# Top-k attention and a hard-swish feed-forward in one kernel: transposing a unit's weights three steps after its scores, and feed-forward pieces of half the size

## Chip, cores and metric

The kernel runs on one core of one Trainium2 chip. The metric is the time on the device in microseconds (us) of one execution. Of a kernel's plain runs the median counts; one more execution is recorded by the profiler, and its own time stands beside it.

TensorE is the matrix engine (PE in the profile, its weight loads PEld), VectorE is DVE, ScalarE is ACT, GpSimd is POOL, and SyncE (SP) issues the transfers.

## What is computed

Attention over 8 batches, 8 heads, 576 positions and a head dimension of 64, where each row keeps the scores that reach its 32nd largest; then a feed-forward on 4608 rows of 512, with 2048 inner columns. All in 32-bit floats (the inputs lie in 64-bit floats for the feed-forward's weights, and the kernel converts these itself).

```python
scores = scale * np.matmul(q, k.transpose(0, 1, 3, 2))
kth = np.partition(scores, -32, axis=-1)[..., -32:-31]
scores = np.where(scores >= kth, scores, -1e9)
attn = np.exp(scores - np.max(scores, axis=-1, keepdims=True))
attn = attn / (np.sum(attn, axis=-1, keepdims=True) + 1e-09)
x = np.matmul(attn, v)            # (B,H,S,D) -> (B*S, H*D)
h = x @ w_in
out = (h * np.clip(h + 3.0, 0.0, 6.0) / 6.0) @ w_out
```

## The kernel before

**Units.** The heads go in pairs, four pairs a batch. A pair's 576 rows are four blocks of 128 rows and a rest of 64. A *full* unit is one block of 128 rows for both heads of a pair: two score tiles of 128 x 576. A *rest* unit is the rest of 64 rows of both heads, which lie above one another in the partitions: one tile of 128 x 576. There are 128 full and 32 rest units, 160 in all, in groups of five: four full ones (one for each pair, the same block) and a rest one, which stands last in even batches and first in odd ones.

**What happens to a unit.** `scores` (L206 for a rest unit, L213 for a full one) multiplies on TensorE into `big`, and ScalarE copies it out (L208, L214, L217). `top` finds the 32 largest of each row on VectorE: four rounds of `max` (L230), with three of `match_replace` (L234) between them, which write the work buffer `wk`. `mask` compares and adds on GpSimd (L244, L249) and makes the shift (L252). `exp` is ScalarE's exponential with its running sum (L257), and GpSimd adds a small constant to the sum, `den` (L262). `weights` takes the reciprocal on VectorE (L266) and scales on ScalarE (L268). `transpose` turns the weights on TensorE into `big` (L279), and ScalarE copies them to `eT` (L281). `values` multiplies with v into a PSUM tile `pv` (L291), for a full unit together with that of the neighbour, and ScalarE copies it out (L409). After the fourth full unit of a group, 128 rows of x are whole and a feed-forward tile is put on the list `todo`; the rest units give one such tile for every two batches. So there are 36 feed-forward tiles.

**Shared buffers.** `big` is one PSUM tile of four banks; scores, weights' transposes and the transposes of a new pair's q and k (`pT` below, L178, L180, copied out at L183, L184) take turns in it. The other four PSUM banks are a pool (`ps_w`) for the feed-forward's `h` and `acc`, for `pv` and for the conversion's `f`. There are four score tiles `sc` and two `wk`.

**Feed-forward in pieces.** A tile of 128 rows is a generator with eight pieces: four that each compute 512 columns of h (16 matmuls, L308), ScalarE's rectifier (L316) and, delayed to the next piece, VectorE's gate (L320); then four that each add four of the sixteen products into `acc` (L327), the last with ScalarE's scaling (L337) and the store. `piece()` runs the next one, if `todo` holds one.

**Order.** The order is written out by hand; each engine works through its list in that order. In step n stand, for TensorE: scores of unit n+1; a piece; transposes of unit n-2; a piece (not if unit n is a rest unit); perhaps a pair's transposes; `values`; and at every fourth step one more piece. For VectorE: the reciprocal of unit n-2, then the four rounds of unit n, with gates between them. For ScalarE: the scaling of unit n-2 behind the copy of the scores of n+1, and the exponential of unit n-1 at the end. For GpSimd: the sum of unit n-1, then the mask of unit n. The first eight steps (EARLY) differ: there a unit is finished one step later, and the weights of the feed-forward are loaded and converted from 64-bit to 32-bit floats (`convert`, L99 to L122), one chunk of 32 at each of four calls in a step. A call finishes the oldest chunk under way if two are, and starts the next. The tile names in this program are the ones that the trace prints.

Of the kernel before, what the change touches and what calls it, by code (L numbers as in the profile page):

```python
# [26 lines left out]
def kernel(  # L27
# [16 lines left out]
    NHP = H // 2  # L44
# [5 lines left out]
    def pool(name, bufs, **kw):  # L50
        return ctx.enter_context(tc.tile_pool(name=name, bufs=bufs, **kw))
# [1 line left out]
    consts = pool("consts", 1)  # L53
    ldpool = pool("ld", 2)
    kqpool = pool("kq", 2 * NHP)
    scpool = pool("sc", 4)
    wkpool = pool("wk", 2)
    mpool = pool("m", 4)
    etpool = pool("et", 2)
# [64 lines left out]
    def weight_chunks():  # L124
        win, wout = moe_w_in.bitcast(U32), moe_w_out.bitcast(U32)
        for f in range(0, FF, WC):
            for g in range(NHP):
                rows = slice(g * P, (g + 1) * P)
                yield w_in[:, g, f : f + WC], win[rows, 2 * f : 2 * (f + WC)]
        for c in range(NFC):  # L130
            rows = slice(c * P, (c + 1) * P)
            yield w_out[:, c, :], wout[rows, :]
# [168 lines left out]
    def feed_forward(xT, rows):  # L301

        gs = []
        for f0 in range(0, NFC, 4):
            h = ps_w.tile([P, 512], F32, tag="w", name="h")
            for f in range(f0, f0 + 4):
                for i in range(NHP):
                    nc.tensor.matmul(  # L308
                        h[:, (f - f0) * P : (f - f0 + 1) * P],
                        w_in[:, i, f * P : (f + 1) * P],  # L310
                        xT[:, i, :],
                        start=(i == 0),
                        stop=(i == NHP - 1),
                    )
            g = gpool.tile([P, 512], F32, tag="g", name="g")
            nc.scalar.activation(g[:], h[:], AF.Relu, bias=three[:], scale=1.0)  # L316
            gs.append(g)

            def gate(g=g, h=h):
                nc.vector.scalar_tensor_tensor(  # L320
                    out=g[:], in0=g[:], scalar=6.0, in1=h[:], op0=ALU.min, op1=ALU.mult
                )

            yield gate
        acc = ps_w.tile([P, DM], F32, tag="w", name="acc")
        for f in range(NFC):
            nc.tensor.matmul(  # L327
                acc[:],
                gs[f // 4][:, (f % 4) * P : (f % 4 + 1) * P],
                w_out[:, f, :],  # L330
                start=(f == 0),
                stop=(f == NFC - 1),
            )
            if f % 4 == 3:
                if f == NFC - 1:
                    o = opool.tile([P, DM], F32, tag="o", name="o")
                    nc.scalar.mul(o[:], acc[:], 1.0 / 6.0)  # L337
                    for p0, p1, dst in rows:
                        nc.sync.dma_start(dst, o[p0:p1, :])
                yield None  # L340
# [5 lines left out]
    pairs = {(b, hp): Pair(b, hp) for b in range(B) for hp in range(NHP)}  # L346
    units = []
    for b in range(B):
        for qt in range(J):
            full = [Unit(pairs[b, hp], qt) for hp in range(NHP)]  # L350
# [3 lines left out]
    per_batch = NHP * (J + 1)  # L354
    NU = len(units)
    todo = []
    gate = None

    def run_gate():
        nonlocal gate  # L360
        if gate:
            gate()
        gate = None

    def piece():
        nonlocal gate
        run_gate()
        while todo:
            try:
                gate = next(todo[0])  # L370
                return
            except StopIteration:
                todo.pop(0)

    chunks = list(weight_chunks())
    converting = []

    def convert_step():

        if converting and (len(converting) > 1 or not chunks):  # L380
            next(converting.pop(0), None)
        if chunks:
            c = convert(*chunks.pop(0))
            next(c)
            converting.append(c)

    EARLY = 8
    state = {}

    def values(n):  # L390
# [30 lines left out]
    def pair_at(n, first):  # L421

        b, at = divmod(n, per_batch)
        hp, odd = divmod(at - first, 3)
        return pairs[b + 1, hp] if b + 1 < B and not odd and 0 <= hp < NHP else None

    pairs[0, 0].load()
    convert_step()
    pairs[0, 0].transpose()
    units[0].scores()  # L430
    convert_step()
    pairs[0, 1].load()
    convert_step()
    pairs[0, 1].transpose()
    for hp in range(2, NHP):
        pairs[0, hp].load()
    for hp in range(NHP):
        pairs[0, hp].load_values()

    for n in range(NU + 2):  # L440
        early = n < EARLY
        u = units[n] if n < NU else None
        pieces = 2
        if u and u.rest:
            pieces = 1
        if n % 4 == 3 and n > 2 * EARLY:
            pieces += 1
        d = n - (1 if early else 2)
        d = d if 0 <= d < NU and n != EARLY else None
        if n + 1 < NU:  # L450
            units[n + 1].scores()
        if n < 2:
            pairs[0, n + 2].transpose()
        if d is not None and not early:
            units[d].weights()
        if u:
            u.begin()
            u.top(0)
        p = pair_at(n, 6)
        if p:  # L460
            p.load()
            p.load_values()
        convert_step()
        piece()
        if u:
            u.top(1)
        if d is not None:
            if early:
                units[d].exp()
            else:  # L470
                units[d].transpose()
        convert_step()
        if u:
            u.top(2)
        convert_step()
        if d is not None and early:
            units[d].weights()
            units[d].transpose()
        if pieces > 1:
            piece()  # L480
        p = pair_at(n, 8)
        if p:
            p.transpose()
        if d is not None:
            values(d)
        if u:
            u.top(3)
        convert_step()
        for _ in range(2, pieces):
            piece()  # L490
        if not early and 1 <= n < NU + 1:
            units[n - 1].exp()
        if u:
            u.mask()
    while todo:
        piece()
    run_gate()


# [32 lines left out]
```

## Time and profile before

| | us |
|---|---|
| median of 3 runs | 1967.45 |
| lowest and highest | 1967.02, 1968.03 |
| the profiled execution | 1967.0 |
| its span, first to last instruction | 1965.2 |

| engine | busy us | share of the span |
|---|---|---|
| TensorE, matmuls | 1688.6 | 86% |
| TensorE, weight loads | 1237.7 | 63% |
| VectorE | 1551.5 | 79% |
| GpSimd | 1160.5 | 59% |
| ScalarE | 973.6 | 50% |

The mean granted clock of TensorE is 0.933 of full speed. A step takes some 11 us. Busy times overlap; what counts is which engine waits for which, and in which stretch. In the chain that ended last, followed back from the end, TensorE has 78% of the span, GpSimd 9% and ScalarE 8%.

### The profile page before, as it was taken

The numbers are of one execution on the slowest core, as the hardware profiler recorded it, in microseconds if no ns is written. First come the engines' busy times: TensorE is split into PE (matmuls) and PEld (weight loads), VectorE is DVE, ScalarE is ACT, GpSimd is POOL, SyncE is SP. The second block draws the span as 40 slices with busy tenths as digits, with TensorE's granted clock in tenths as the row PEclk, the third lists the DMA queues.
The fourth block names the chain that finished last, engine by engine and source line by source line (L and its number), as shares of the span: only waits on it lengthen the run. The fifth ranks groups of instructions, "written<-read, shape, count | busy, mean of one in ns | idle before, by whom it ended". The sixth has DMA issues, their size and how long they took to land.

```text
span 1965.2 us, 30832 instructions
## 1 busy us (share of the span) xinstructions
PE 1688.6 (86%) x11872; PEld 1237.7 (63%) x11872; DVE 1551.5 (79%) x3249; ACT 973.6 (50%) x1717; POOL 1160.5 (59%) x878
## 2 busy tenths in 40 slices
PE   3346889788999998798899998988899999978899
PEld 2244666556777766566666766666576666665576
DVE  4775897877988777888898778887898888877860
ACT  3553465455554554544544555544554554454541
POOL 3875665656656555665665556555566565555650
PEclk9877899889999999898899999988899999988899
DMA  6340100110001100101001110001001010000000
GB/s 180 117 126 27 45 7 7 42 33 15 1 24 31 39 10 6 43 12 31 7 6 25 30 42 7 25 18 42 7 6 25 25 42 7 6 7 6 6 7 11
DMA packets 101139, 56.53 MB, mean 29 GB/s; under 512 B 84096, under 2 KB 92288, under 8 KB 100992
## 3 DMA queue, kind: packets, MB, share of 16 engines
q1 hardware_dynamic: 100992, 54.55, 10.2%
q8 instruction: 94, 1.54, 0.3%
q14 instruction: 53, 0.43, 0.1%
HBM read 45.09 MB, written 9.44 MB: 28 GB/s over the span
## 4 chain that ended last, share of the span: by engine, by line
PE 78%; POOL 9%; ACT 8%; issue 3%; SPq 1%; DMA 1%; DVE 1%; POOLq 0%; ACTq 0%
PE h L308 26%; PE acc L327 23%; PE pv L291 10%; PE big L279 8%; PE big L213 6%; POOL wk L244 5%; POOL sc L249 3%; ACT sc L257 2%; ACT eT L281 2%; PE big L206 2%; PE big L178 2%; ACT kq L183 1%; ACT sc L214 1%; ACT sc L268 1%; DMA st<-in_moe_w_in_dram 0%
## 5 line engine op out<-in xcount | busy, mean ns | idle before, releaser
L244 POOL TENSOR_SCALAR wk<-sc,m 128x576 f32<-128x576 f32 x288 | 638.1, 2223 | 30.7 <-DVE m L230 19.8
L230 DVE MAX8 m<-wk 128x8 f32<-128x576 f32 x864 | 620.5, 762 | 3.0
L327 PE MATMUL acc<-w_out,g 128*128 128x512 f32 x1152 | 527.8, 603 | 0.0
L308 PE MATMUL h<-xT,w_in 128*128 128x128 f32 x4096 | 488.6, 278 | 0.0
L308 PEld LDWEIGHTS h<-xT,w_in 128*128 128x128 f32 x4096 | 470.2, 193 | 6.2 <-issue 1.3
L234 DVE MATCH_REPLACE8 wk<-m,wk 128x576 f32<-128x576 f32 x576 | 427.4, 756 | 0.0
L262 POOL TENSOR_SCALAR den<-den 128x2 f32<-128x2 f32 (+1 forms) x160 | 37.4, 234 | 632.5 <-ACT sc L257 595.4
L249 POOL TENSOR_TENSOR sc<-sc,wk 128x1152 f32<-128x1152 f32 (+1 forms) x160 | 382.3, 2389 | 13.3
L327 PEld LDWEIGHTS acc<-w_out,g 128*128 128x128 f32 x1152 | 210.5, 192 | 222.7 <-issue 217.0
L279 PE MATMUL big<-ident,sc 128*128 128x128 f32 x1344 | 201.2, 297 | 168.8 <-ACT sc L268 136.3
L279 PEld LDWEIGHTS big<-ident,sc 128*128 128x128 f32 x1344 | 169.4, 154 | 212.6 <-issue 143.1
L257 ACT ACTIVATE sc<-sc,shift 128x576 f32<-128x576 f32 x288 | 221.4, 772 | 118.3 <-POOL shift L252 118.1
L266 DVE RECIPROCAL den<-den 128x2 f32<-128x2 f32 (+1 forms) x160 | 26.5, 165 | 296.3 <-POOL den L262 296.0
L281 ACT COPY eT<-big 128x1152 f32<-128x1152 f32 (+1 forms) x160 | 169.1, 1057 | 128.9 <-PE big L279 128.9
L316 ACT ACTIVATE g<-h,three 128x512 f32<-128x512 f32 x144 | 99.2, 689 | 268.4 <-PE h L308 268.3
L268 ACT ACTIVATE sc<-sc,den 128x576 f32<-128x576 f32 x288 | 210.8, 778 | 26.0 <-DVE den L266 24.8
L213 PE MATMUL big<-kq 64*128 64x512 f32 (+1 forms) x1024 | 182.3, 478 | 40.7 <-ACT eT L281 25.4
L234 DVE MATCH_REPLACE8 wk<-m,sc 128x576 f32<-128x576 f32 x288 | 212.9, 750 | 0.0
L291 PE MATMUL pv<-eT,vm 128*64 128x128 f32 (+1 forms) x2560 | 186.6, 296 | 25.4 <-ACT eT L281 25.4
L230 DVE MAX8 m<-sc 128x8 f32<-128x576 f32 x288 | 204.1, 749 | 3.6 <-ACT sc L217 3.6
L291 PEld LDWEIGHTS pv<-eT,vm 128*64 128x64 f32 x2560 | 156.0, 156 | 60.2 <-ACT eT L281 32.7
L213 PEld LDWEIGHTS big<-kq 64*128 64x128 f32 x1024 | 95.5, 202 | 141.1 <-issue 88.5
(42 smaller groups left out, 1074.6 us busy)
## 6 DMA issues: line engine op xcount, KB each, us to landing
kin<-in_k_dram SPq DMA_DIRECT2D x64, 128.0 KB, 2.9
qin<-in_q_dram SPq DMA_DIRECT2D x64, 128.0 KB, 2.8
st<-in_moe_w_in_dram SPq DMA_DIRECT2D x16, 512.0 KB, 4.2
vm<-in_v_dram SPq DMA_DIRECT2D x64, 128.0 KB, 2.4
st<-in_moe_w_out_dram SPq DMA_DIRECT2D x16, 512.0 KB, 3.7
out_dram<-o SPq DMA_DIRECT2D x32, 256.0 KB, 2.2
rest<-in_k_dram SPq DMA_DIRECT2D x32, 32.0 KB, 2.5
rest<-in_q_dram SPq DMA_DIRECT2D x32, 32.0 KB, 2.6
```

Source lines behind the costliest of these rows:

```text
L213: nc.tensor.matmul(banks[:, 2 * i + hh, 0 : s1 - s0], pr.qT[d, qs], pr.kT[d, s0:s1])
L230: nc.vector.max(self.m[:, t, 8 * r : 8 * r + 8], self.cur[t])
L234: nc.vector.match_replace(wk, self.m[:, t, 8 * r : 8 * r + 8], self.cur[t], LOWEST)
L244: nc.gpsimd.tensor_scalar(self.wk[:, t, :], self.row[t], self.m[:, t, TOP_K - 1 : TOP_K], DROP, ALU.is_lt, ALU.mult,)
L249: nc.gpsimd.tensor_tensor(both, both, self.wk[:, 0:nt, :].rearrange("p t s -> p (t s)"), ALU.add)
L257: nc.scalar.activation(self.row[t], self.row[t], AF.Exp, bias=self.shift[:, t : t + 1], scale=scale, accum_out=self.den[:, t : t + 1],)
L268: nc.scalar.activation(self.row[t], self.row[t], AF.Copy, scale=self.den[:, t : t + 1])
L279: nc.tensor.transpose(ps[:, i * P : (i + 1) * P], self.sc[:, c0 : c0 + P], ident[:])
L281: nc.scalar.copy(eT[:, 0:n, :].rearrange("p c q -> p (c q)"), ps[:, 0 : n * P])
L291: nc.tensor.matmul(dst[hh * D : (hh + 1) * D, :], pr.vm[:, hh, c, :] if c < J else pr.vr[:, hh, :], rhs, start=(c == 0), stop=(c == J),)
L308: nc.tensor.matmul(h[:, (f - f0) * P : (f - f0 + 1) * P], w_in[:, i, f * P : (f + 1) * P], xT[:, i, :], start=(i == 0), stop=(i == NHP - 1),)
L327: nc.tensor.matmul(acc[:], gs[f // 4][:, (f % 4) * P : (f % 4 + 1) * P], w_out[:, f, :], start=(f == 0), stop=(f == NFC - 1),)
```

## The change

The transposes of a unit's weights, with the reciprocal and the scaling ahead of them, come three steps after its round of `top` and not two (LAG = 3), from step 10 on; a fifth score tile holds the unit that waits. The exponential stays where it was. A feed-forward tile has sixteen pieces of half the size: h of two column blocks, or two of the sixteen products. A step of a full unit runs two halves ahead of the transposes, one behind them, and one behind a pair's transposes; a rest unit's step one ahead and one behind; every fourth step two more at the end. A gate runs two halves after its h is whole. In the startup, the loads of the third and fourth pair and the values of all pairs come later and one by one, and three chunks of the conversion are under way instead of two.

```diff
-    scpool = pool("sc", 4)
+    scpool = pool("sc", 5)
...
             for f in range(f0, f0 + 4):
+                if f == f0 + 2:
+                    yield None
...
-            if f % 4 == 3:
+            if f % 2 == 1:
...
-    gate = None
...
-    def piece():
-        nonlocal gate
-        run_gate()
-        while todo:
-            try:
-                gate = next(todo[0])
-                return
-            except StopIteration:
-                todo.pop(0)
+    gates = []
+
+    def piece(count=1):
+        for _ in range(count):
+            while todo:
+                try:
+                    gates.append(next(todo[0]))
+                    break
+                except StopIteration:
+                    todo.pop(0)
+            else:
+                gates.append(None)
+            if len(gates) > 2:
+                gate = gates.pop(0)
+                if gate:
+                    gate()
...
-    def convert_step():
-
-        if converting and (len(converting) > 1 or not chunks):
+    def convert_step(depth=1):
+
+        if converting and (len(converting) > depth or not chunks):
...
+    LAG = 3
...
-    convert_step()
+    convert_step(2)
     pairs[0, 0].transpose()
     units[0].scores()
-    convert_step()
+    convert_step(2)
     pairs[0, 1].load()
-    convert_step()
     pairs[0, 1].transpose()
-    for hp in range(2, NHP):
-        pairs[0, hp].load()
-    for hp in range(NHP):
-        pairs[0, hp].load_values()
-
-    for n in range(NU + 2):
+    convert_step(2)
+    pairs[0, 2].load()
+    pairs[0, 0].load_values()
+    pairs[0, 1].load_values()
+
+    for n in range(NU + LAG):
...
-        d = n - (1 if early else 2)
-        d = d if 0 <= d < NU and n != EARLY else None
+        full = not (u and u.rest)
+        d = n - (1 if early else LAG)
+        d = d if 0 <= d < NU and (early or d >= EARLY - 1) else None
+        depth = 2 if n < 3 else 1
...
+        if n == 0:
+            pairs[0, 3].load()
+        if n in (1, 2):
+            pairs[0, n + 1].load_values()
...
-        convert_step()
-        piece()
+        convert_step(depth)
+        piece(2 if full else 1)
...
-        convert_step()
+        piece()
+        convert_step(depth)
         if d is not None and early:
             units[d].weights()
             units[d].transpose()
-        if pieces > 1:
             piece()
         p = pair_at(n, 8)
         if p:
             p.transpose()
+        if full and not early:
+            piece()
...
-        for _ in range(2, pieces):
-            piece()
+        convert_step(depth)
+        if n % 4 == 3 and n > 2 * EARLY:
+            piece(2)
```

**ScalarE, from the exponential of unit 109 on** (a full unit, ahead of the rest unit 110). `sc` is a unit's score tile, so the number tells the unit. Before:

```order
L257 ACTIVATE sc_9464,den_9681<-sc_9464,shift_9637 128x576 x2
L214 COPY sc_9690<-big_9689 128x2x512
L217 COPY sc_9690<-big_9689 128x128
L268 ACTIVATE sc_9464<-sc_9464,den_9681 128x576 x2
L281 COPY eT_9710<-big_9711 128x1152
```

Now:

```order
L257 ACTIVATE sc_9401,den_9655<-sc_9401,shift_9591 128x576 x2
L214 COPY sc_9664<-big_9663 128x2x512
L217 COPY sc_9664<-big_9663 128x128
L268 ACTIVATE sc_9312<-sc_9312,den_9587 128x576 x2
L281 COPY eT_9688<-big_9689 128x1152
L183 COPY kq_9706<-big_9707 128x2x512
L184 COPY kq_9706<-big_9707 128x2x64
L339 ACTIVATE o_9721<-acc_9579 128x512
L257 ACTIVATE sc_9510,den_9726<-sc_9510,shift_9659 128x576
L214 COPY sc_9735<-big_9734 128x2x512
L217 COPY sc_9735<-big_9734 128x128
L268 ACTIVATE sc_9401<-sc_9401,den_9655 128x576 x2
```

Before, the scaling of the same unit (L268) follows its exponential (L257) with one copy of scores between them; now it is the scaling of the unit before that, and the unit's own comes after the next exponential.

**TensorE, steps 106 and 107.** Each step begins with two rows of scores (L213). Before:

```order
L213 MATMUL big<-kq 128x512 x2
L213 MATMUL big<-kq 128x64 x2
L279 MATMUL big<-ident,sc 128x128 x9
L291 MATMUL pv<-eT,vm_126 64x128 x8
L291 MATMUL pv<-eT,vr_127 64x128 x2
L291 MATMUL pv<-eT,vm_123 64x128 x8
L291 MATMUL pv<-eT,vr_124 64x128 x2
L213 MATMUL big<-kq 128x512 x2
L213 MATMUL big<-kq 128x64 x2
L308 MATMUL h<-xT,w_in 128x128 x16
L279 MATMUL big<-ident,sc 128x128 x6
L308 MATMUL h<-xT,w_in 128x128 x16
```

Now:

```order
L213 MATMUL big<-kq 128x512 x2
L213 MATMUL big<-kq 128x64 x2
L279 MATMUL big<-ident,sc 128x128 x9
L213 MATMUL big<-kq 128x512 x2
L213 MATMUL big<-kq 128x64 x2
L279 MATMUL big<-ident,sc 128x128 x9
L291 MATMUL pv<-eT,vm_126 64x128 x8
L291 MATMUL pv<-eT,vr_127 64x128 x2
L291 MATMUL pv<-eT,vm_123 64x128 x8
L291 MATMUL pv<-eT,vr_124 64x128 x2
L310 MATMUL h<-xT,w_in 128x128 x16
```

In the kernel before, the `values` of that step complete 128 rows of x, and step 107 begins with a piece of h; now they stand in step 107, so that steps 106 and 107 both go without a piece until their end.

**SyncE, in the startup,** where the feed-forward's weights begin to be loaded in a row. Before (behind all loads of q, k and v of the first batch):

```order
L162 DMA vm_114<-in_v_dram 128x256
L166 DMA vr_115<-in_v_dram 64x64
L100 DMA st<-in_moe_w_in_dram 128x1024 x13
L100 DMA st<-in_moe_w_out_dram 128x1024 x11
L150 DMA kin<-in_k_dram 128x4x64 x2
```

Now (behind the values of the first two pairs):

```order
L150 DMA kin<-in_k_dram 128x4x64 x2
L154 DMA rest<-in_k_dram 64x2x64
L150 DMA qin<-in_q_dram 128x4x64 x2
L154 DMA rest<-in_q_dram 64x2x64
L100 DMA st<-in_moe_w_in_dram 128x1024 x4
L162 DMA vm_111<-in_v_dram 128x256
L166 DMA vr_112<-in_v_dram 64x64
```

The values of the third and fourth pair went behind the first four and eight of these weight loads.

## Rows read from the trace of the kernel before

**Rows 1.** Part 1 of the page: busy us of each engine, share, instructions

```profile
PE 1688.6 (86%) x11872; PEld 1237.7 (63%) x11872; DVE 1551.5 (79%) x3249; ACT 973.6 (50%) x1717; POOL 1160.5 (59%) x878
```

**Rows 2.** Windows: stretch, length; busy PE, PEld, DVE, ACT, POOL; clock, DMA, GB/s

```profile
0.00:226.80 226.80, 111.79 (x681) 84.23 (x682) 149.46 (x301) 103.71 (x183) 141.22 (x134) 0.83 0.36 105
...
989.30:1178.80 189.50, 182.22 (x1277) 130.03 (x1276) 152.91 (x323) 96.97 (x170) 110.15 (x81) 0.98 0.10 26
1178.80:1446.40 267.60, 234.52 (x1694) 174.98 (x1693) 225.32 (x476) 136.81 (x244) 163.67 (x121) 0.92 0.07 19
1333.60:1343.10 9.50, 4.84 (x23) 2.50 (x22) 5.57 (x11) 5.75 (x11) 7.49 (x5) 0.97 0.40 101
...
1425.00:1474.00 49.00, 49.00 (x369) 37.83 (x368) 44.58 (x95) 27.02 (x49) 32.51 (x22) 1.00 0.02 6
```

**Rows 3.** Waits, 246 to 1965 us: who, for whom, total us, times, longest

```profile
DVE den L266 <- POOL den L262: 278.3, 94, 11.8
...
PE big L279 <- ACT sc L268: 79.4, 20, 4.9
...
PE pv L291 <- ACT eT L281: 21.8, 18, 1.2
PE big L213 <- ACT eT L281: 21.8, 18, 1.2
...
PEld acc L327 <- DVE wk L234: 1.5, 7, 0.2
```

**Rows 4.** Timeline of step 110: start, us, engine, operation [idle before <- releaser]

```profile
1333.65 4.41 POOL L244 TENSOR_SCALAR wk<-sc,m 128x576 f32<-128x576 f32 x2
...
1338.15 2.62 POOL L249 TENSOR_TENSOR sc<-sc,wk 128x1152 f32<-128x1152 f32 x1
...
1341.13 0.78 ACT L257 ACTIVATE sc<-sc,shift 128x576 f32<-128x576 f32 x1 [2.83 <-POOL shift L252]
...
1343.10 0.17 DVE L266 RECIPROCAL den<-den 128x2 f32<-128x2 f32 x1 [3.73 <-POOL den L262]
...
1344.59 2.15 PE L279 MATMUL big<-ident,sc 128*128 128x128 f32 x9 [4.94 <-ACT sc L268]
```

**Rows 5.** Timeline, TensorE at full clock, 1367 to 1374 us

```profile
1367.51 1.30 PE L213 MATMUL big<-kq 64*128 64x512 f32 x8
...
1368.74 3.84 PE L308 MATMUL h<-xT,w_in 128*128 128x128 f32 x32
...
1372.41 1.15 PE L279 MATMUL big<-ident,sc 128*128 128x128 f32 x9
...
1373.39 3.60 PE L327 MATMUL acc<-w_out,g 128*128 128x512 f32 x8
```

**Rows 6.** Timeline, 1186 to 1197 us: scores, exponential's end, mask, scaling

```profile
1186.88 1.30 PE L213 MATMUL big<-kq 64*128 64x512 f32 x8
...
1188.54 0.19 ACT L257 ACTIVATION_READ_ACCUMULATOR sc<-sc,shift 128x1 f32 x1
...
1189.13 4.41 POOL L244 TENSOR_SCALAR wk<-sc,m 128x576 f32<-128x576 f32 x2
...
1189.68 1.45 ACT L268 ACTIVATE sc<-sc,den 128x576 f32<-128x576 f32 x2
...
1193.63 2.64 POOL L249 TENSOR_TENSOR sc<-sc,wk 128x1152 f32<-128x1152 f32 x1
```

**Rows 7.** Timeline of the startup, SyncE's issues and VectorE's waits

```profile
25.72 0.58 SPq L162 DMA_DIRECT2D vm<-in_v_dram  x1
...
30.38 40.13 SPq L100 DMA_DIRECT2D st<-in_moe_w_in_dram  x13
...
36.26 1.48 DVE L115 TENSOR_SCALAR a<-a 128x512 uint32<-128x512 uint32 x1 [9.98 <-POOL a L107]
...
107.75 0.43 DVE L115 TENSOR_SCALAR a<-a 128x512 uint32<-128x512 uint32 x1 [5.57 <-POOL a L107]
...
194.90 0.17 DVE L266 RECIPROCAL den<-den 128x2 f32<-128x2 f32 x1 [11.91 <-POOL den L262]
```

More of the change, by code (lines that the diff above doesn't have):

```diff
@@ L356 @@
     todo = []
-    gate = None
-    def run_gate():
-        nonlocal gate
-        if gate:
-            gate()
-        gate = None
-    def piece():
-        nonlocal gate
-        run_gate()
-        while todo:
-            try:
-                gate = next(todo[0])
-                return
-            except StopIteration:
-                todo.pop(0)
+    gates = []
[13 more added lines that the diff above has]
+                    gate()
     chunks = list(weight_chunks())
     converting = []
-    def convert_step():
-        if converting and (len(converting) > 1 or not chunks):
+    def convert_step(depth=1):
+        if converting and (len(converting) > depth or not chunks):
             next(converting.pop(0), None)
@@ L427 @@
     pairs[0, 0].load()
-    convert_step()
+    convert_step(2)
     pairs[0, 0].transpose()
     units[0].scores()
-    convert_step()
+    convert_step(2)
     pairs[0, 1].load()
-    convert_step()
     pairs[0, 1].transpose()
-    for hp in range(2, NHP):
-        pairs[0, hp].load()
-    for hp in range(NHP):
-        pairs[0, hp].load_values()
-    for n in range(NU + 2):
+    convert_step(2)
[3 more added lines that the diff above has]
+    for n in range(NU + LAG):
         early = n < EARLY
         u = units[n] if n < NU else None
[L443 to L447, printed above, removed]
-        d = n - (1 if early else 2)
-        d = d if 0 <= d < NU and n != EARLY else None
+        full = not (u and u.rest)
+        d = n - (1 if early else LAG)
+        d = d if 0 <= d < NU and (early or d >= EARLY - 1) else None
+        depth = 2 if n < 3 else 1
         if n + 1 < NU:
@@ L471 @@
                 units[d].transpose()
-        convert_step()
+        convert_step(depth)
         if u:
             u.top(2)
-        convert_step()
+        piece()
+        convert_step(depth)
         if d is not None and early:
@@ L487 @@
             u.top(3)
-        convert_step()
-        for _ in range(2, pieces):
-            piece()
+        convert_step(depth)
+        if n % 4 == 3 and n > 2 * EARLY:
+            piece(2)
         if not early and 1 <= n < NU + 1:
@@ L496 @@
         piece()
-    run_gate()
+    piece(2)
 _INS = ["q", "k", "v", "moe_w_in", "moe_w_out"]
```

## The prediction

> **What bounds the kernel now.** The page's share of busy time comes first [rows 1]: TensorE 86%, VectorE 79%. Both are high and neither is full, so the question is which waits for which, and where. The windows [rows 2] split the span. Until 226.8 us (steps 0 to 11, weights still being converted) TensorE works 111.8 us. After that the program repeats every 40 steps, with two kinds of stretch. In steps 80 to 95 (989.3 to 1178.8 us) TensorE is busy 182.2 of 189.5 us: it sets the pace. I call that a full stretch. In steps 96 to 119 (1178.8 to 1446.4 us) it is busy 234.5 of 267.6 us, VectorE 225.3, at a mean clock of 0.92: neither is full. I call that a thin stretch, because the feed-forward runs out of pieces there (below).
>
> The waits [rows 3] say what holds VectorE: 278.3 us, in 94 waits, in front of the reciprocal, for GpSimd's `den`. And TensorE: 79.4 us in front of the transposes of the weights (L279), for ScalarE's scaling by 1/den (L268), plus 1.2 us stalls, 18 times each, of `values` (L291, 21.8 us) and of scores (L213, 21.8 us) behind the copy that empties `big`. The timeline of step 110, whose unit is a rest unit [rows 4], shows why the first wait exists. Unit 109's mask starts on GpSimd at 1333.65, its sum starts at 1338.15, its exponential at 1341.13, and only at 1343.10 does VectorE get the reciprocal, having waited 3.73 us; TensorE's transposes start at 1344.59 after 4.94 us of idleness. The step lasts 9.5 us though VectorE works only 5.57 in it [rows 2]. So a rest step is set by the chain mask, exponential, sum, reciprocal of the unit before it, because that unit's weights are asked for one step after its mask. There are 32 rest units.
>
> In a full step the same reciprocal ties VectorE to TensorE from the other side: the exponential stands on ScalarE behind the copy of `values`, so VectorE can't start step n before TensorE has ended step n-1.
>
> **The change part by part.** *Lag three.* The reciprocal of step n is now that of unit n-3, whose exponential was issued a full step earlier; the chain of [rows 4] leaves VectorE's path. What is late next is the work buffer `wk`, of which there are two: step n writes the one of unit n-2, whose mask must have ended. That mask stands on GpSimd behind the sum of unit n-3, and that behind its exponential. From [rows 6]: the exponential ends at 1188.73 (1188.54 + 0.19), the next mask starts at 1189.13 and its last part ends at 1193.63 + 2.64 = 1196.27, so 7.5 us after the exponential. VectorE needs the buffer some 1.4 us into a step, so it may start step n about 6 us after the exponential issued in step n-2, where before it had to start after that issued in step n-1. (Behind the new wait would stand the rest of the step on VectorE, its gates too, and so TensorE's acc pieces.) That gains one TensorE step less 5.5 us: about 5 us in a full-size step (11 us), nothing in one of 5.5. The trace of before never shows this wait, as the other one hides it: its price per rest step lies between 0 and the 3.9 us (9.50 - 5.57) that the step waits now; I take near 0, since GpSimd works 163.7 of 267.6 us in the thin stretch [rows 2]. The fifth score tile that the lag needs costs room only.
>
> *TensorE's work* is unchanged. At full clock a scores group advances TensorE by 1.23 us (1367.51 to 1368.74), a feed-forward piece of h by 3.67, a unit's transposes by 0.98 [rows 5]. Halving a piece adds 288 boundaries. [Rows 5] show none that costs anything (the transposes follow at once); bounds 0 and 0.1 us each (29 us), and I take 0.
>
> *Halves between uses of `big`.* A half (1.8 us) now lies behind the transposes in rest steps too, and one behind the pair's transposes. The copy that empties `big` takes about 1.2 us of waiting, so a half covers it. In thin steps with no pieces left, the stall stays.
>
> *Where pieces run out.* Counting pieces through the program's loop, both kernels have 82 places (of full size) in 40 steps for 72 pieces. Before, the empty places are scattered by one or two. After, in the thin 24 steps, ten are empty, in steps that correspond to 101, 106, 107, 111, 112 and 117, and 106 and 107 are wholly empty before `values`. In the four steps with nothing ahead of the transposes, the scaling by 1/den still stands on ScalarE behind the copy of the scores: from the start of scores at 1186.88 to the end of scaling (1189.68 + 1.45 = 1191.13) are 4.25 us [rows 6], of which scores fill 1.23, so about 2.8 to 3 us of TensorE idle remain in each: 4 x 2.8 = 11. To these come six stalls of 1.2 behind `big`: 7. The rest of the idle time goes, because VectorE can now be up to 5 us early.
>
> *Thin stretch.* TensorE's work at full clock: the mean clock 0.92 means 16% of 267.6 = 43 us at half clock; 33.1 us of the stretch are idle. If all idleness lies in the slow 43 us, 10 us of work ran slow and lost 5; if none does, 43 did and lost 21. So the work is 213 to 229 us; I take 222, as the slow patches hold both. After: 222 + 11 + 7 + 1 of leftover waits + 7.5 lost to the clock (before 12.5; fewer and shorter gaps) = 248.5, against 267.6: 19 us saved. Ends: 228 (waits nearly all hidden) and 261 (waits 28, clock 11). Steps 20 to 159 hold 92 such steps, 3.83 stretches: **73 us** (25 to 152).
>
> *Full stretch.* 7.3 us idle and about 2 of clock; the halves in rest steps cover most of it: 7 each, three of them: **21 us** (12 to 27). Steps 12 to 19 likewise: **5**.
>
> *Startup.* The load of pair 3 and the values of pairs 2 and 3 move behind the conversions' loads on SyncE's queue. Before, thirteen weight loads were issued from 30.38 us on and VectorE stood 9.98 us for the first, until 36.26 [rows 7]; now the values of pairs 2 and 3, whose last eight issues took from 25.72 to 30.38, 4.7 us, are no longer ahead, and VectorE finishes a chunk three calls after its start, not two. Against that a chunk that was finished before step 0 moves into it (1.1). Step 0 saves about 7 us (4 to 9). The deeper pipeline also eases waits like 5.57 us at 107.75: I take 8 of about 24 left (0 to 18). The 11.91 us ahead of the reciprocal at 194.90 turn into the `wk` wait: 4 saved. Against that, the second feed-forward tile comes a step later, which leaves two pieces (7.3) and a unit's transposes and values, 9 in all, for TensorE's later time. 7 + 8 + 4 - 9: net **10 us** (0 to 28). The tail is TensorE's own work in both.
>
> *Sum.* 1965.2 - 73 - 21 - 5 - 10 = 1856.2 of span. The profiled execution took 1967.0 with a span of 1965.2, so 1.8 lie around it: 1858. Its own 1967.0 is 0.45 under the median of the runs, which I neglect.
>
> **A rule of the skill weighed.** The traced row first: in 1425 to 1474 us, at clock 1.00, matmuls fill 49.00 of 49.00 us while weight loads fill 37.83 [rows 2]. So TensorE had no room there. The Trainium skill, page "Perfetto Trace Analysis", section "Identifying the Most-Contended Engine", holds that matmul busy time is a poor measure of TensorE's headroom and that the busy share of the weight loads is a better one. By that share (63% on [rows 1]) VectorE, at 79%, would be the bound, and the time would be rival D's; by the rows it is the forecast's, and the stretch speaks against the page here.
>
> **Rivals.**
> A, *the `wk` wait takes the place.* If GpSimd's mask ends late after every exponential, VectorE waits there as long as before. It decides where TensorE's step is 5.5 us or less, as thin steps are. For it: the mask chain of 7.5 us is most of a step. Against: GpSimd is 61% busy. Left are the startup (10) and half of the 44 us of stalls behind `big` [rows 3]: 1967 - 32 = 1935 us.
> B, *thin steps stay thin.* The emptied steps now lie side by side, the gaps drop the clock as before, and the stretch takes 257: 10.6 x 3.83 = 41 saved; with 21, 5 and 10: 1890 us.
> C, *slower: banks for h.* A tile h keeps one of four PSUM tiles over two halves and two more until its gate. If TensorE then waits for a gate at each of 144 tiles, for as long as one half takes (1.83), that is 264 us on top: 2122. It decides from 109/144 = 0.8 us a tile. Against: at most two h, one acc and one `values` tile are alive, and TensorE's loads waited for VectorE there only 1.5 us in 7 times [rows 3].
> D, *VectorE sets the pace*: its 278 us of waits vanish entirely: 1689 us. Against: TensorE's 1688.6 busy us [rows 1] would have to leave no gap, or matmuls to overlap more than in [rows 2].
>
> **How the numbers follow.** Chances: forecast 0.67, A 0.12, B 0.13, C 0.05, D 0.03. The predicted time is the forecast's 1858. The range reaches over B and most of the bounds: 1800 (thin stretch at about 233) to 1905; outside lie A, C and D, 0.20. The measurement tells 0.2% (4 us) from nothing. Faster: forecast, B, D and nearly all of A, 0.94; same 0.01; slower 0.05.
>
> **What would show it.** Right: waits for `den` on VectorE down from 278 us to a few tens; rest steps of 6 to 8 us in thin stretches; no stalls of `values` and scores behind `big` outside steps without pieces; TensorE's mean clock above 0.95; VectorE's first match-replace of a step as a new waiter, for GpSimd's L249, under 40 us in all; step 0 some 7 us shorter. Wrong: long waits of match-replace for the mask (A), thin stretches near 257 with clock 0.92 (B), waits of h's first matmul for a gate (C). The forecast fails if idle time in thin stretches is tied to ScalarE's queue rather than to VectorE's reciprocal, more than the four steps that I count.

## The result, and the profile after

The changed kernel takes 1866.3 us (median of 4 runs, 1863.4 to 1867.1) where the kernel before takes 1967.2: the ratio is 0.9484, with a 95% interval of 0.9468 to 0.9501. The prediction said 1858, range 1800 to 1905. The profiled execution took 1863.4 us, its span 1861.6, so 103.6 us of span are gone.

First the page of the changed kernel: busy us of each engine, the chain that ended last by engine, and of the costliest groups that of h (busy us, mean ns | idle us ahead, its releaser).

```profile
PE 1671.3 (90%) x11872; PEld 1217.5 (65%) x11872; DVE 1549.7 (83%) x3249; ACT 969.4 (52%) x1717; POOL 1157.0 (62%) x878
...
PE 83%; ACT 7%; POOL 6%; issue 2%; SPq 1%; DVE 1%; DMA 0%; ACTq 0%; POOLq 0%
...
L310 PE MATMUL h<-xT,w_in 128*128 128x128 f32 x4096 | 491.6, 278 | 12.5 <-DVE y L116 10.7
```

Beside [rows 1] VectorE's and GpSimd's busy time hardly moved; the span shrank around them. TensorE's fell by 17 us, since less of its work ran at half clock. Its share of the chain rose from 78% to 83%.

The windows of the changed kernel, for the stretches that [rows 2] shows of before: steps 0 to 11, 80 to 95, 96 to 119, and the rest step 110; then steps 106 and 107. Columns: stretch, length; busy time (and instructions) of PE, PEld, DVE, ACT, POOL; clock, DMA share, GB/s.

```profile
0.00:207.00 207.00, 96.50 (x546) 69.65 (x548) 148.83 (x300) 98.12 (x172) 138.59 (x132) 0.82 0.39 113
927.20:1102.30 175.10, 173.32 (x1257) 126.20 (x1256) 152.96 (x323) 96.20 (x171) 110.70 (x82) 1.00 0.11 27
1102.30:1357.30 255.00, 237.80 (x1713) 173.17 (x1712) 224.93 (x477) 136.57 (x244) 162.82 (x119) 0.95 0.08 20
1251.70:1257.50 5.80, 5.12 (x24) 2.58 (x23) 5.53 (x14) 4.09 (x9) 3.96 (x6) 1.00 0.00 0
1202.90:1224.40 21.50, 14.42 (x99) 10.22 (x100) 19.46 (x44) 11.98 (x20) 15.12 (x12) 0.70 0.38 96
```

The full stretch is 14.4 us shorter (189.5 to 175.1) and has no slow clock left. The thin one is 12.6 shorter (267.6 to 255.0), and its TensorE idles 17.2 us (255.0 - 237.8) where it idled 33.1. Step 110 lasts 5.8 us, not 9.5. What is left of the old picture stands in steps 106 and 107: 7.1 of 21.5 us idle, mean clock 0.70.

The waits of the changed kernel, 200 to 1861 us: who, for whom, total us, times, longest.

```profile
DVE wk L234 <- POOL sc L249: 104.7, 51, 5.1
DVE g L322 <- ACT g L318: 101.0, 38, 16.6
...
PE big L279 <- ACT sc L268: 36.9, 17, 2.6
...
DVE den L266 <- POOL den L262: 20.2, 5, 12.4
PE pv L291 <- ACT eT L281: 16.9, 14, 1.2
...
PE big L213 <- ACT eT L281: 5.1, 4, 1.3
```

Against [rows 3], the wait for `den` fell from 278.3 us to 20.2, and TensorE's wait for the scaling from 79.4 to 36.9. A new one is the first here: VectorE's match-replace waits 104.7 us for GpSimd's mask.

The timeline of step 110 in the changed kernel (start, us, engine, operation, [idle before <- releaser]), to hold against [rows 4]:

```profile
1249.57 2.63 POOL L249 TENSOR_TENSOR sc<-sc,wk 128x1152 f32<-128x1152 f32 x1
...
1251.66 0.17 DVE L266 RECIPROCAL den<-den 128x2 f32<-128x2 f32 x1
...
1252.55 0.78 ACT L257 ACTIVATE sc<-sc,shift 128x576 f32<-128x576 f32 x1 [2.63 <-POOL shift L252]
...
1256.01 1.38 PE L279 MATMUL big<-ident,sc 128*128 128x128 f32 x9 [0.68 <-issue]
```

Unit 109's exponential starts at 1252.55, so after the step's reciprocal (1251.66): that reciprocal is unit 107's, and waits for nothing. TensorE's idle time ahead of the transposes is 0.68 us, where it was 4.94.

### The profile page after: what moved, and what is told of

It is laid out like the page before. It is cut to its first block, busy times and chain, and to the rows that moved or that the text cites. A ratio compares the mean times of both kernels' runs of the same rounds, so it can differ in the third digit from the quotient of the medians.

```text
span 1861.6 us, 31024 instructions
## 1 busy us (share of the span) xinstructions
PE 1671.3 (90%) x11872; PEld 1217.5 (65%) x11872; DVE 1549.7 (83%) x3249; ACT 969.4 (52%) x1717; POOL 1157.0 (62%) x878
## 3 DMA queue, kind: packets, MB, share of 16 engines
q1 hardware_dynamic: 100992, 54.55, 10.7%
## 4 chain that ended last, share of the span: by engine, by line
PE 83%; ACT 7%; POOL 6%; issue 2%; SPq 1%; DVE 1%; DMA 0%; ACTq 0%; POOLq 0%
PE h L310 28%; PE acc L329 25%; PE pv L291 10%; PE big L279 9%; PE big L213 7%; POOL wk L244 3%; POOL sc L249 2%; PE big L206 2%; ACT sc L257 2%; PE big L178 2%; ACT eT L281 2%; ACT sc L214 1%; ACT sc L268 1%; ACT a L106 1%; DMA st<-in_moe_w_in_dram 0%
## 5 line engine op out<-in xcount | busy, mean ns | idle before, releaser
L244 POOL TENSOR_SCALAR wk<-sc,m 128x576 f32<-128x576 f32 x288 | 637.1, 2220 | 14.4
L310 PE MATMUL h<-xT,w_in 128*128 128x128 f32 x4096 | 491.6, 278 | 12.5 <-DVE y L116 10.7
L329 PEld LDWEIGHTS acc<-w_out,g 128*128 128x128 f32 x1152 | 206.3, 190 | 204.7 <-issue 199.7
L279 PE MATMUL big<-ident,sc 128*128 128x128 f32 x1344 | 198.4, 292 | 117.3 <-ACT sc L268 91.3
L279 PEld LDWEIGHTS big<-ident,sc 128*128 128x128 f32 x1344 | 163.6, 150 | 169.9 <-issue 109.8
L257 ACT ACTIVATE sc<-sc,shift 128x576 f32<-128x576 f32 x288 | 220.6, 769 | 50.2 <-POOL shift L252 49.8
L268 ACT ACTIVATE sc<-sc,den 128x576 f32<-128x576 f32 x288 | 210.4, 777 | 2.6 <-DVE den L266 2.6
L291 PE MATMUL pv<-eT,vm 128*64 128x128 f32 (+1 forms) x2560 | 178.5, 287 | 19.3 <-ACT eT L281 19.3
L213 PE MATMUL big<-kq 64*128 64x512 f32 (+1 forms) x1024 | 178.7, 470 | 17.1 <-ACT eT L281 8.7
L291 PEld LDWEIGHTS pv<-eT,vm 128*64 128x64 f32 x2560 | 148.1, 150 | 58.1 <-ACT eT L281 38.7
L322 DVE SCALAR_TENSOR_TENSOR g<-g,h 128x512 f32<-128x512 f32 x144 | 99.0, 687 | 102.4 <-ACT g L318 102.4
L213 PEld LDWEIGHTS big<-kq 64*128 64x128 f32 x1024 | 93.9, 198 | 132.9 <-issue 96.6
```

The source lines that it names most:

```text
L213: nc.tensor.matmul(banks[:, 2 * i + hh, 0 : s1 - s0], pr.qT[d, qs], pr.kT[d, s0:s1])
L244: nc.gpsimd.tensor_scalar(self.wk[:, t, :], self.row[t], self.m[:, t, TOP_K - 1 : TOP_K], DROP, ALU.is_lt, ALU.mult,)
L257: nc.scalar.activation(self.row[t], self.row[t], AF.Exp, bias=self.shift[:, t : t + 1], scale=scale, accum_out=self.den[:, t : t + 1],)
L268: nc.scalar.activation(self.row[t], self.row[t], AF.Copy, scale=self.den[:, t : t + 1])
L279: nc.tensor.transpose(ps[:, i * P : (i + 1) * P], self.sc[:, c0 : c0 + P], ident[:])
L291: nc.tensor.matmul(dst[hh * D : (hh + 1) * D, :], pr.vm[:, hh, c, :] if c < J else pr.vr[:, hh, :], rhs, start=(c == 0), stop=(c == J),)
```

## The experiments

The forecast's theory: what the kernel gained, it gained because VectorE no longer waits for the sum of the unit before, and TensorE now sets the pace nearly everywhere; what is left is lost where pieces run out. The runs below test this. Each ratio is against the kernel before.

**The parts alone.** Lag three with five score tiles, on the kernel before:

```diff
-    scpool = pool("sc", 4)
+    scpool = pool("sc", 5)
...
+    LAG = 3
...
-    for n in range(NU + 2):
+    for n in range(NU + LAG):
...
-        d = n - (1 if early else 2)
-        d = d if 0 <= d < NU and n != EARLY else None
+        d = n - (1 if early else LAG)
+        d = d if 0 <= d < NU and (early or d >= EARLY - 1) else None
```

> The kernel before with the lag of three steps and the fifth score tile alone; pieces stay whole, the startup stays. Theory (the reciprocal of the unit two steps back is what ties VectorE to the mask chain and to TensorE): VectorE's waits for den (278 us in the steady part before, 20 after the whole change) fall below 40 us, rest steps shrink from 9.5 us to 6 or 7, and the lag brings the larger part of the 101 us: 1880 to 1905 us. Rival (the halves between uses of the shared tile are what counts): the waits for den fall, but TensorE then stands behind the shared tile instead, and no more than 30 us come: 1937 us or more.

Measured: 1892.5 us, ratio 0.9628 (0.9615 to 0.9641): 73.6 us less. Its waits, 200 us to the end:

```profile
DVE wk L234 <- POOL sc L249: 118.7, 66, 5.0
...
PE pv L291 <- ACT eT L281: 33.8, 28, 1.2
...
DVE den L266 <- POOL den L262: 22.0, 5, 12.4
```

The wait for `den` goes with the lag; the stalls of `values` behind `big` stay, and even grow beyond those of [rows 3].

Halves with their new places, and the rest as before (against the changed kernel; the startup's loads stand as before too):

```diff
-    scpool = pool("sc", 5)
+    scpool = pool("sc", 4)
...
-    LAG = 3
+    LAG = 2
...
-        depth = 2 if n < 3 else 1
+        depth = 1
...
```

> The kernel before with the half pieces and their new places alone; lag of two steps, four score tiles, startup of before. Theory: waits of VectorE for den stay above 200 us and rest steps stay at 9.5 us; half of the 44 us of stalls of values and scores behind the shared tile goes, 10 to 25 us: 1942 to 1957 us. Rival (the halves count most): 1915 us or less.

Measured: 1945.5 us, ratio 0.9892 (0.9879 to 0.9906): 20.7 us less, with a wait for `den` of 265.6 us that is nearly untouched. Scores' stalls behind `big` fall from 21.8 to 4.8 us.

The startup's loads and its three chunks under way, alone (on the kernel before, in part):

```diff
-    for hp in range(2, NHP):
-        pairs[0, hp].load()
-    for hp in range(NHP):
-        pairs[0, hp].load_values()
+    pairs[0, 2].load()
+    pairs[0, 0].load_values()
+    pairs[0, 1].load_values()
...
+        depth = 2 if n < 3 else 1
...
```

> The kernel before with the startup alone: later loads of pairs 3 and 4 and of the values, three chunks of the conversion under way. Theory: step 0 is 7 to 8 us shorter (24.7 before, 16.8 after the whole change), little else moves, and the time falls by 6 to 12 us: 1955 to 1961 us. Rival (the startup's gain is eaten by TensorE, which sets the later pace): step 0 is as short, but the time is within 4 us of 1967.

Measured: 1962.2 us, ratio 0.9983 (0.9974 to 0.9992): 3.9 us under the kernel before, which lies between the two expectations; its eleven runs lie from 1961.2 to 1965.9 us, so the 3.9 is itself loose. Step 0 is 7.4 us shorter (24.66 to 17.23), but steps 5 to 7 take 6.1 longer (61.0 to 67.1): most of the gain is lost again there. The three parts alone sum to 98.2 us, the whole change gives 100.9: they hardly help or hinder one another.

**Is the new wait of match-replace worth anything?** A third work buffer in the changed kernel:

```diff
-    wkpool = pool("wk", 2)
+    wkpool = pool("wk", 3)
```

> The changed kernel with a third work buffer wk. It takes away the new wait of the change, that of VectorE's match-replace for GpSimd's L249 (104.7 us in 51 waits from 200 us on). Theory (TensorE sets the pace, the wait is VectorE's slack): the wait disappears, VectorE's next wait (for the copy of the scores, or for den) takes most of it, and the time stays at 1866 us within 8 us. Rival (this wait has taken the old one's place and still binds): half of it or more is won, 1815 us or less.

Measured: 1864.9 us, ratio 0.9484 (0.9471 to 0.9497), the changed kernel's own. Its waits, 200 us to the end:

```profile
DVE g L322 <- ACT g L318: 186.4, 62, 16.6
...
DVE den L266 <- POOL den L262: 28.8, 9, 12.4
```

The 104.7 us are gone from the list, and 85.4 us of them stand one line further on, as waits of the gate for TensorE's h by way of ScalarE (101.0 to 186.4). So the wait was VectorE's slack: it is ahead, and waits for TensorE in the one place or the other. Rival A falls here.

**TensorE's wait for the scaling.** The reciprocal and the scaling go ahead of the scores' copy on ScalarE:

```diff
+        if d is not None and not early:
+            units[d].weights()
         if n + 1 < NU:
             units[n + 1].scores()
...
-        if d is not None and not early:
-            units[d].weights()
```

> The changed kernel with the reciprocal and the scaling by 1/den issued ahead of the next scores' copy on ScalarE instead of behind it. Theory (in the four steps of a thin stretch with no piece ahead of the transposes, TensorE stands 2.6 us each for the scaling, which stands behind the copy of the scores on ScalarE): TensorE's waits for L268 (36.9 us in 17 waits) fall to under 20 us, and 8 to 20 us are won: 1846 to 1858 us. Rival (these waits are VectorE's, not ScalarE's queue): 1862 us or more.

A miss: 1872.8 us, ratio 0.9528 (0.9514 to 0.9542), 6.5 us slower than the changed kernel. Its wait list says why:

```profile
PE big L279 <- ACT sc L217: 40.9, 17, 3.2
```

The wait for L268 (36.9 us, 17 times) became one for L217, 17 times: the transposes write `big`, so they need the copy that empties it as well as the scaled weights. Both stand on ScalarE, and the order of the two decides which is named. Waits for the rest units' copy (L208, 4.8 us, 4 times) come on top, so the transposes wait 8.8 us more in all, of the order of the 6.5 us lost.

**Do empty places cost what is left?** In the changed kernel 82 places of full size (164 halves) stand against 72 pieces in 40 steps. Without the two halves at every fourth step, there are 144 places for 144 halves:

```diff
-        if n % 4 == 3 and n > 2 * EARLY:
-            piece(2)
```

> The changed kernel without the two extra halves at every fourth step, so that places and pieces are 144 and 144 in 40 steps, and no step runs out of pieces from step 38 on. Theory (what is left above TensorE's own work, some 400 us at full clock in 40 steps against 430 measured, is lost in the steps that run out of pieces, as idleness and as half clock): 40 steps take 403 to 412 us, the mean clock rises above 0.97 in the steady part, three such periods win 54 to 80 us, of which a longer feed-forward tail may take a few back: 1790 to 1815 us. Rival (VectorE and its waits set the pace by now): 1845 us or more.

Measured: 1778.7 us, ratio 0.9050 (0.9037 to 0.9064), better than expected and 88 us below the changed kernel. Its window for steps 80 to 119 (columns as above):

```profile
890.20:1295.70 405.50, 399.26 (x2970) 291.96 (x2969) 376.68 (x797) 232.03 (x413) 273.51 (x201) 1.00 0.10 24
```

Forty steps take 405.5 us, all at full clock, where the same steps of the changed kernel take 430.1. TensorE fills 98% of them. The Trainium skill, page "Perfetto Trace Analysis", section "Identifying the Most-Contended Engine", takes the weight loads' share for the truer measure of TensorE's headroom; that is 72% here (291.96 of 405.5), under VectorE's 93%. The third work buffer below tells which of them sets the pace.

The scaling first, on top of that:

```diff
+        if d is not None and not early:
+            units[d].weights()
         if n + 1 < NU:
             units[n + 1].scores()
...
-        if d is not None and not early:
-            units[d].weights()
...
-        if n % 4 == 3 and n > 2 * EARLY:
-            piece(2)
```

> Both at once: no extra halves, and the scaling ahead of the copy of the scores. Theory: with no step without a piece ahead of its transposes, the scaling's place no longer matters, and the time is that of the kernel without extra halves within 6 us. Rival (ScalarE's order costs in every step): 8 us or more below it.

A miss as well: 1790.5 us, ratio 0.9109 (0.9094 to 0.9124), 11.8 us above the even pieces. A reading, not shown by a run of its own: a unit's scaling is two instructions, and with the scaling last the transposes begin behind the first of them (in the trace of the even lag of four below, L268 x2 runs from 1237.25 to 1238.70, the transposes start at 1238.13). With the copy last they must wait for all of it. TensorE's idle time ahead of the transposes fits: in the rest step 110 it is 1.51 us with the scaling first, 0.87 with the scaling last.

**A third work buffer again,** now that no step runs short and VectorE is 87% busy over the whole span:

```diff
-    wkpool = pool("wk", 2)
+    wkpool = pool("wk", 3)
...
-        if n % 4 == 3 and n > 2 * EARLY:
-            piece(2)
```

> Even pieces with a third work buffer. The wait of VectorE's first match-replace for GpSimd's mask (87 us with two) should vanish. If TensorE sets the pace, the time stays within 5 us of 1778.7. If with no step short of pieces VectorE (87% busy) has become the next limit, the wait is worth part of its 87 us: 1720 to 1765 us.

Measured: 1779.7 us, ratio 0.9049 (0.9034 to 0.9064): nothing. The wait for the mask (87.1 us) vanishes, the gate's wait rises from 50.2 to 129.5. TensorE still sets the pace, so the trace speaks against the page's measure here: its matmuls' 98% told the truth, and not the 72% of the weight loads.

**Is three the right lag?** The changed kernel with a lag of four and a sixth score tile:

```diff
-    scpool = pool("sc", 5)
+    scpool = pool("sc", 6)
-    LAG = 3
+    LAG = 4
```

> The changed kernel with a lag of four steps and six score tiles. Theory (after the lag of three VectorE is held by the work buffer wk and TensorE by its own work, no longer by the reciprocal: 20 us of waits left): nothing to win, 1860 to 1872 us. Rival (the slack between VectorE and TensorE is still what is short): 1850 us or less.

The largest miss: 1918.9 us, ratio 0.9762 (0.9748 to 0.9777), 52.6 us slower than the changed kernel, though the waits for `den` are gone. My first thought was that x comes a step later and the tiles meet other empty places. So lag four with even pieces, and in the same way lag two with four score tiles:

```diff
-    scpool = pool("sc", 5)
+    scpool = pool("sc", 6)
...
-    LAG = 3
+    LAG = 4
...
-        if n % 4 == 3 and n > 2 * EARLY:
-            piece(2)
```

> Even pieces with a lag of four steps and six score tiles. A lag of four made the changed kernel 52 us slower, with TensorE idle in steps without a piece. If that loss came from which steps run out of pieces (x is whole a step later, so the tiles come at other steps), no step runs out here and the time is within 12 us of the 1778.7 of the even pieces: 1767 to 1791 us. If the lag itself costs (the later values, the order on ScalarE or GpSimd), the loss stays: 1815 to 1835 us.

> Even pieces, but the transposes two steps after the scores again, with four score tiles (LAG = 2). In the changed kernel the lag gave about 74 us of its 101. If the lag is worth that only where steps run out of pieces (TensorE's step shorter than VectorE's chain), most of its gain is gone here, since no step runs out: 1785 to 1815 us, and the waits for den stay under 150 us. If every rest step needs the lag, whatever its pieces, the whole gain is missing: 1840 to 1865 us, waits for den above 200 us.

Lag four: 1836.8 us, ratio 0.9340 (0.9327 to 0.9354), so the loss stays (58 us), and the thought was wrong. Lag two: 1838.8 us, ratio 0.9349 (0.9335 to 0.9363), nearly the time of the second case. Its waits for `den` are at the bound of the first (149.9 us up to 1770 us, 159.2 to the end), and its rest steps last 9.5 us again. The lag is worth 60 us even where no step runs short.

Three beats two and four by nearly the same sum. For four the timeline shows why. Lag four, TensorE, ScalarE and GpSimd behind a rest unit's transposes (columns as above):

```profile
1231.69 2.62 POOL L249 TENSOR_TENSOR sc<-sc,wk 128x1152 f32<-128x1152 f32 x1
1231.73 1.30 PE L213 MATMUL big<-kq 64*128 64x512 f32 x8
...
1232.95 3.84 PE L310 MATMUL h<-xT,w_in 128*128 128x128 f32 x32
...
1234.67 0.78 ACT L257 ACTIVATE sc<-sc,shift 128x576 f32<-128x576 f32 x1 [2.15 <-POOL shift L252]
...
1236.21 0.99 ACT L214 COPY sc<-big 128x1024 f32<-128x1024 f32 x1
...
1237.25 1.45 ACT L268 ACTIVATE sc<-sc,den 128x576 f32<-128x576 f32 x2
1238.13 1.39 PE L279 MATMUL big<-ident,sc 128*128 128x128 f32 x9 [1.34 <-issue]
```

The exponential waits 2.15 us for a full unit's mask on GpSimd; the scores' copy and the scaling stand behind it on ScalarE; TensorE ends its two halves and idles 1.34 us. The same place with even pieces and a lag of three:

```profile
1200.47 2.64 POOL L249 TENSOR_TENSOR sc<-sc,wk 128x1152 f32<-128x1152 f32 x1
1200.51 1.09 PE L291 MATMUL pv<-eT,vm 128*64 128x128 f32 x16
...
1202.84 1.30 PE L213 MATMUL big<-kq 64*128 64x512 f32 x8
...
1203.47 0.78 ACT L257 ACTIVATE sc<-sc,shift 128x576 f32<-128x576 f32 x1
...
1207.74 1.15 PE L279 MATMUL big<-ident,sc 128*128 128x128 f32 x9
```

Here `values` of two units (2.3 us, from 1200.51 to 1202.84) keep TensorE busy during the mask. `values` are issued for two neighbours at once, at the second. With a lag of three the unit that is transposed in a rest unit's step is (but for changes of batch) such a second one; with two or four it is a first one, and nothing covers the mask. The test puts another cover there: one half moves from the step behind to the rest unit's.

```diff
-        if full and not early:
+        after_rest = full and 0 < n <= NU and units[n - 1].rest
+        if not early and not after_rest:
             piece()
```

> Even pieces with a lag of four: one half moves from the step behind a rest unit's to the end of the rest unit's step. The trace of the even lag of four shows TensorE idle for 1.34 to 1.47 us ahead of the transposes in the step behind each rest unit's (at 1238.13, for example), while ScalarE's exponential waits for GpSimd's shift with the copy of the scores and the scaling queued behind it; with a lag of three the values (2.3 us of TensorE) stand in the rest unit's step and cover this, with four they don't. If that is the cause, half a piece (1.83 us) covers it too: some 30 such steps at 1.4 us, 42 us less than 1836.8, so 1787 to 1806 us. If the lag of four costs elsewhere, 1825 us or more.

Measured: 1788.2 us, ratio 0.9096 (0.9081 to 0.9111): 48.6 us come back. The start of step 159 is at 1686.1 us, with a lag of three at 1686.6; most of the 9.5 us that remain stand in the tail, which is 99.5 us against 92.0. So the loss of lag four was for the most part the missing cover.

For lag two this is not shown. TensorE does idle in the same place, behind a rest unit's step and for as long, but there the old chain still runs, as VectorE's wait for `den` tells:

```profile
1250.41 0.77 ACT L257 ACTIVATE sc<-sc,shift 128x576 f32<-128x576 f32 x1 [3.51 <-POOL shift L252]
...
1252.37 0.17 DVE L266 RECIPROCAL den<-den 128x2 f32<-128x2 f32 x1 [3.26 <-POOL den L262]
...
1253.86 1.39 PE L279 MATMUL big<-ident,sc 128*128 128x128 f32 x9 [1.55 <-issue]
```

The late exponential is that of the unit whose weights are asked for next, as in [rows 4]. Whether a cover alone would bring the 60 us back was not tried.

Of all these, the even pieces (1778.7 us) are the fastest; the third work buffer adds nothing to them.

## Why the prediction was right, and where its terms were not

**The mechanism holds.** The lag takes the wait for `den` off VectorE (278.3 to 20.2 us), 23 of the 32 rest steps take 5.75 to 7.1 us (predicted 6 to 8; the others 8.9 to 9.9, and one in the startup 15.9), and TensorE sets the pace. The lag alone gives 73.6 of the 100.9 us.

**Four terms,** by the starts of steps in the two traces. To step 12: 19.8 us saved (226.8 to 207.0); predicted 7 + 8 + 4 = 19. Steps 12 to 19: 6.3 (83.4 to 77.1); predicted 5. Steps 20 to 158: 89.0 (1575.2 to 1486.2); predicted 94. From the start of step 159 to the end: 11.5 *longer* (79.8 to 91.3), with 561 matmuls there instead of 451. I had 9 us for work that the later tile leaves, but set them against the startup and said that the tail stays; the lag alone has the longer tail too (91.9), halves alone and the startup alone have not (79.8 each). Sum 103.6 of span, predicted 109.

**Two of them are right by errors that cancel.** The 94 were 73 from thin stretches and 21 from full ones. Measured, a thin one gives 12.6 (I took 19.1) and a full one 14.4 (I took 7): 3.83 x 12.6 + 3 x 14.4 = 91. The step that was wrong is the work and the clock that I put into the thin stretch, 222 us plus 7.5.

The work first. The windows are cut where VectorE starts a step, and TensorE is not at the same place then. The scores with which it begins step 96, and VectorE's start of that step, in the kernel before and then in the changed one:

```profile
1176.92 1.30 PE L213 MATMUL big<-kq 64*128 64x512 f32 x8
1178.81 1.40 DVE L230 MAX8 m<-sc 128x8 f32<-128x576 f32 x2
...
1102.35 0.76 DVE L230 MAX8 m<-sc 128x8 f32<-128x576 f32 x1
1106.30 1.30 PE L213 MATMUL big<-kq 64*128 64x512 f32 x8
```

TensorE was 1.9 us ahead of VectorE there and is now 4.0 behind; at step 80 it is 0.8 further behind than before. So some 5 us of its work fall into the thin window that fell into the full one. The counts agree: 1277 matmuls in the full stretch before and 1257 after, 1694 in the thin one before and 1713 after. This part only moves time between the two windows, and cancels in the sum.

The clock next. The even pieces' forty steps hold the same 2970 matmuls in 399.3 busy us at clock 1.00. Less the 173.3 of the changed full stretch, the thin one's work is some 226 us, an estimate; its 237.8 busy us then hold 11.8 lost to the clock, where I had 7.5. Before, by the same reckoning, it held 234.5 - 221 = 13.5: the gaps became fewer, but the clock's loss hardly fell. What I said of idleness was close: 17.2 us against 11 + 7 + 1 = 19. So 226 + 11.8 + 17.2 = 255.0 stand where I had 222 + 7.5 + 19 = 248.5. In the full stretch I had too little: besides the 5 us moved, its idle time fell from 7.3 to 1.8 us and all of the clock's loss went.

The 82 places, and steps 106 and 107 without a piece, stand in the trace of the changed kernel:

```profile
1208.16 1.30 PE L213 MATMUL big<-kq 64*128 64x512 f32 x8
1212.00 2.15 PE L279 MATMUL big<-ident,sc 128*128 128x128 f32 x9 [2.55 <-ACT sc L268]
1215.42 2.40 PE L213 MATMUL big<-kq 64*128 64x512 f32 x8 [1.26 <-ACT eT L281]
1219.87 2.15 PE L279 MATMUL big<-ident,sc 128*128 128x128 f32 x9 [2.06 <-ACT sc L268]
1223.23 1.97 PE L291 MATMUL pv<-eT,vm 128*64 128x128 f32 x16 [1.21 <-ACT eT L281]
```

Waits of 2.55 and 2.06 us for the scaling (predicted 2.8 to 3) and stalls of 1.2 behind `big`, as predicted; behind the first gap the work runs at half clock (scores take 2.40 us, not 1.30).

**The startup** is right in its sum, with other parts. Step 0 gained 7.9 (predicted 7). The deeper pipeline, for which I took 8, shows no gain of its own: alone, the startup's edit, loads and depth together, has 2.3 of its 7.4 us left at step 8. In the whole change steps 5 to 7 don't give them back (61.4 us, before 61.0). The halves alone take 57.9 us there and the lag alone 61.5, so it is probably the halves; startup and halves without the lag were not run. By step 20 the lag alone is 11.3 us ahead, halves alone 7.8, the startup alone 4.4, the whole 26.1. Steps 8 to 11, where the lag sets in, fell from 53.5 to 43.0 us, with the lag alone to 47.0; I had counted 4 there.

**The halves** cost next to nothing at their boundaries: with even pieces TensorE is idle 6.24 of 405.5 us, over 72 added boundaries, so under 0.09 us each. Stalls of scores fell from 21.8 to 5.1 us. Those of `values` fell only to 16.9: they are left where pieces run out.

**The `wk` wait** was mis-sized: 104.7 us, where I had said under 40. I took it for a cost, and judged its size by how busy GpSimd is; it is where a VectorE that is ahead happens to wait, and a third buffer moves it without gain.

**The rivals.** A and D fall by the third work buffer: VectorE waits for the mask and does not pay for it, nor does it set the pace. B named the right place: the thin stretch took 255, nearer to its 257 than to my 248.5, though at clock 0.95 and not 0.92, and the full ones made up for it. C does not occur: h waits 12.5 us in all, 10.7 of them for the conversion in the startup, with the four PSUM tiles as they are.

**The clock** is 0.95, at the bound that I gave, not above it; with even pieces it is 0.975.

## What to carry to other kernels

The longest wait in the list need not be the dearest: give it a buffer, and if the same time turns up in another line and the run takes as long, its engine is only ahead. Count the places for filler work against the filler work, since surplus places bunch the empty ones; making them equal was worth 88 us here, nearly as much as the whole change. And a lag is not only a distance: it decides which work stands beside which wait. Four steps were 58 us slower than three here, until half a piece, put where the cover was missing, brought back 48.6 of them.
